# Two batches' states, loaded early and turned on TensorE: one DMA transpose replaced in a hand-ordered kernel

## The chip, the cores and the metric

The kernel runs on one core of a Trainium2 chip. The core has five engines with a queue of their own each: PE (TensorE, the products; its weight loads are shown apart as PEld), DVE (VectorE), ACT (ScalarE), POOL (GpSimd) and SP (SyncE, which here only issues DMAs). The metric is the device time of one execution in microseconds (us), lower is better; of several runs the median is given.

## The reference, cut to what matters

Attention in both directions between a sequence x and a small state, for 8 batches and 8 heads, and behind it a two-layer block with a leaky ReLU:

```python
B, H, S, Ns, D = (8, 8, 512, 32, 64)
scores  = scale * x @ state.T      # per batch and head: 512 x 32
a       = softmax(scores)          # over the 32 state rows
xread   = a @ state
scores2 = scale * state @ x.T      # 32 x 512
a2      = softmax(scores2)         # over the 512 positions
sread   = a2 @ x
rows    = concatenate([xread, sread], axis=2)   # 544 rows a batch, 512 columns (heads side by side)
h       = rows @ w_in              # 4352 x 512 by 512 x 2048
out     = maximum(0.01 * h, h) @ w_out          # 2048 -> 512
```

## The kernel before, in words

**Layout.** The two products `xread = a @ state` and `xread @ w_in` are not made one after the other. For each batch the kernel first makes M = state @ w_in (`a_m`, line 381: heads times states on 256 rows, 2048 columns, in four chunks of 512 columns, each of eight small products), and then h = relu(a @ M) (`ff1`, line 411, 16 blocks j of 128 columns). For both it needs the states transposed, with the head dimension D on the partitions, two heads beside each other: `st_of` (line 214) picks the piece of `stbd` (batch 0), `st1` (batch 1), `st_t[0]` (batches 2 and 3) or `st_t[1]` (batches 4 to 7). The scores (`a_scores`, line 221) are products of the same transposed states with the transposed x (`xT`).

**States.** Batches 0 and 1 are loaded at the start as one DMA of 1-KB rows (`st0f`, line 63: four state rows a partition), scaled, and turned by `state01` (line 157): products whose second operand is a set of columns picked from the identity (`identg`), so that the result stands turned and in the order that the later products want, and two copies on ACT. Batches 2 and 3 (and 4 to 7) go another way: `load_state` (line 177) issues eight DMAs on SP with rows of 256 bytes, and `state_t` (line 186) scales them on POOL and turns them by a DMA transpose on SP into `st_t`. For batches 2 and 3 the load is issued at line 1126, behind a memset on DVE (line 1088) that holds it back, and `state_t(0)` stands at line 1146.

**The head.** x[0] comes in four DMAs, two on SP and two on ACT (line 69), the weights and x[1], x[2] in DMAs issued by POOL. A few products on a tile of zeros (`spin`, line 140) run on PE while the first data come. Batch 0's softmax is made in two halves u = 0, 1 of 256 positions each (`scores0`, `max0`, `rows0`, `split0`, `spread0`, `exp0`, `sum0`, `recip0`, `probs0`, lines 889 to 971). `max0(u, v)` is a reduction on DVE; the negated maxima are split into two bf16 parts (hi, lo) and added to the scores by products; ACT takes the exponential. Then `Quad` (line 1035) makes batch 0's h in half-width blocks, and `piece` (line 693) batch 0's second layer. From batch 1 on, the second layer runs in seven products instead of eight on sums of operands (`Fast`, line 738), whose units are spread between the other work by `before.run(1)` or `u`.

**What sets the order.** The kernel is under a manual schedule: each engine takes its instructions in just the order in which the program writes them, and waits in that order. Lines 973 to 1264 write the order from the start to batch 2 out by hand, `FIRST` (line 1353) that of batch 2's stretch, as a string of short names, and `ORDER` (line 1342) that of batches 3 to 6. So a step that is moved past another changes what is queued behind what. The PSUM banks are handed out by tags with a fixed number of buffers ("big" and "sc" one, "ph" and "py" two): a product that takes a bank waits until the last reader of its former tile is done.

**Around the change.** On PE, line 1179 makes chunk 3 of batch 1's M and line 1182 chunk 0 of batch 2's M, the first product on `st_t[0]`. Batch 1's softmax runs on DVE and ACT from line 1145 (`a_top`, `a_rows`, `a_less`, `a_exp`, `a_max2`, `a_probs`). x[2] and x[3] are cast to bf16 by `cast_x` on ACT and POOL and turned by DMA transposes on SP (`a_xt_dma`, line 208). POOL also makes some of the sums of second-layer weights (`weights_sum`, line 729).

## Time and profile before

| | us |
|---|---|
| median of 3 runs | 201.35 (201.06 to 201.36) |
| the profiled execution | 201.61 |
| its span, first to last instruction | 199.8 |
| PE busy | 193.8 |
| DVE busy | 164.8 |
| ACT busy | 150.1 |
| POOL busy | 63.9 |

How to read the rows that follow. In the order of time a row is: start, duration, engine, line of the kernel, operation, tile written <- tiles read, shape written <- shape read, count; in brackets the idle time of the engine before it and what ended it. `SPq` or `POOL ... DMA_DIRECT2D` rows are the issues of DMAs, not their transfer. A row of the waits is: engine and line <- what it waited for: us in total, times, longest. A row of the DMA issues is: tiles, queue, kind, count, KB in all (a group's mean of one where x8 stands: 16.0 KB each), and the median us from issue to landing. Products are pipelined, so a PE row's duration runs beyond the start of the next; from start to start a product of 512 columns takes 0.22 us here.

### The profile page before, as it was taken

What the parts mean: (1) busy time and instruction counts of PE and PEld (TensorE: products, weight loads), DVE (VectorE), ACT (ScalarE), POOL (GpSimd) and SP (SyncE); (2) the same over time, 40 slices, a digit from 0 to 9 for tenths busy, and PEclk for the clock granted to TensorE, in tenths of its full rate; (3) what the DMA queues carried; (4) which work ended last, traced back from release to release, by engine and by line L of the source; (5) the groups of instructions that cost most, each with busy time, mean ns of one, the idle gap of its engine ahead of it and who ended that gap; (6) DMA issues with size and microseconds to landing.
All of it is one profiled execution on the core that took longest, in us unless ns stands there. A gap on an engine that the chain in (4) does not pass through costs nothing.

```text
span 199.8 us, 5151 instructions
## 1 busy us (share of the span) xinstructions
PE 193.8 (97%) x2106; PEld 136.5 (68%) x2106; DVE 164.8 (82%) x282; ACT 150.1 (75%) x286; POOL 63.9 (32%) x90
## 2 busy tenths in 40 slices
PE   7999998999999999999999999999999999999993
PEld 2566533446677667767777777777777788799882
DVE  2676498599999998997999899999899877995613
ACT  3478628599779649997899779996999768767710
POOL 8473284790009102720413040500050024005350
PEclk9999999999999999999999999999999999999999
DMA  6999997999571998398293614080013401310026
GB/s 203 212 207 192 199 292 136 206 318 162 101 220 27 197 276 165 58 255 268 51 259 113 184 22 85 3 262 0 3 51 159 82 3 76 134 56 0 5 82 182
DMA packets 40616, 27.50 MB, mean 138 GB/s; under 512 B 25424, under 2 KB 37840, under 8 KB 40592
## 3 DMA queue, kind: packets, MB, share of 16 engines
q1 hardware_dynamic: 34032, 20.35, 39.7%
q0 software_dynamic: 5728, 6.03, 16.8%
q10 hardware_dynamic: 832, 0.79, 1.2%
q8 instruction: 16, 0.26, 0.6%
q14 instruction: 8, 0.07, 0.1%
HBM read 17.30 MB, written 8.91 MB: 131 GB/s over the span
## 4 chain that ended last, share of the span: by engine, by line
PE 90%; DMA 4%; DVE 3%; POOL 0%; issue 0%; ACT 0%; ACTq 0%
PE yq L770 43%; PE ph L414 18%; PE pm L393 4%; PE pf L492 3%; PE yu L770 3%; PE pl L660 3%; PE ph L1051 3%; DMA st_t<-stb 2%; DMA xf<-in_x_dram 2%; PE py L699 2%; PE pl L581 2%; PE pyw L699 1%; PE psn L359 1%; PE sc L225 1%; PE php L1051 1%; PE phw L427 1%
## 5 line engine op out<-in xcount | busy, mean ns | idle before, releaser
L420 ACT ACTIVATE hT<-ph 128x512 bf16<-128x512 f32 x84 | 49.1, 608 | 14.3 <-PE ph L414 14.3
L770 PEld LDWEIGHTS <-su 128*128 128x128 bf16 x480 | 46.2, 98 | 12.4 <-ACT hT L420 0.4
L414 PE MATMUL ph<-aT,M 128*128 128x512 bf16 x168 | 47.9, 379 | 0.0
L770 PEld LDWEIGHTS <-hT 128*128 128x128 bf16 x336 | 32.3, 98 | 12.0 <-issue 2.7
L770 PE MATMUL yq<-tw_xf,su 128*128 128x256 bf16 x224 | 30.8, 273 | 0.0
L770 PE MATMUL yq<-w_out_bf,hT 128*128 128x256 bf16 x224 | 29.2, 273 | 0.0
L114 POOL CAST xb<-xl 128x512 bf16<-128x512 f32 (+1 forms) x24 | 15.2, 673 | 20.9 <-DMA xl<-in_x_dram 20.9
L414 PEld LDWEIGHTS <-M 128*128 128x128 bf16 x168 | 16.0, 98 | 7.7 <-issue 1.9
L759 DVE TENSOR_TENSOR su<-hT 128x1024 bf16<-128x1024 bf16 x28 | 19.1, 686 | 2.6 <-ACT hT L420 2.5
L842 POOL TENSOR_TENSOR yo<-sv,sv 128x512 f32<-128x512 f32 x7 | 9.3, 1330 | 37.2 <-ACT e L313 31.4
L1283 ACT CAST M<-pm 128x512 bf16<-128x512 f32 x30 | 16.8, 596 | 0.6 <-PE pm L393 0.6
L779 ACT COPY sv<-yq 128x512 f32<-128x512 f32 x24 | 14.0, 587 | 3.4 <-PE yq L770 3.3
L770 PE MATMUL yq<-tw_x,su 128*128 128x256 bf16 x112 | 16.3, 273 | 0.0
L770 PE MATMUL yq<-w_out_bf,su 128*128 128x256 bf16 x112 | 15.3, 273 | 0.0
L782 DVE TENSOR_TENSOR yo<-yq,sv 128x512 f32<-128x512 f32 x20 | 13.5, 677 | 2.1 <-PE yq L770 2.1
L770 PE MATMUL yq<-tw_x,hT 128*128 128x256 bf16 x104 | 13.9, 273 | 0.0
L313 ACT ACTIVATE e<-sc,mcol 128x512 bf16<-128x512 f32 x16 | 11.2, 704 | 0.2 <-DVE mcol L307 0.2
L699 PEld LDWEIGHTS <-hT 128*128 128x128 bf16 x64 | 5.9, 98 | 7.4 <-issue 0.9
L759 DVE TENSOR_TENSOR su<-su,hT 128x1024 bf16<-128x1024 bf16 x14 | 10.6, 755 | 0.2
L672 ACT COPY ls<-pl 128x512 f32<-128x512 f32 x16 | 9.5, 592 | 1.5 <-PE pl L660 1.0
L307 DVE TENSOR_REDUCE mcol<-sc 128x2 f32<-128x1024 f32 x8 | 9.7, 1216 | 0.0
L235 DVE TRANSPOSE_TENSOR_REDUCE mrow<-sc 128x32 f32<-128x1024 f32 x7 | 8.7, 1243 | 0.5 <-PE sc L225 0.5
(193 smaller groups left out, 350.8 us busy)
## 6 DMA issues: line engine op xcount, KB each, us to landing
xl<-in_x_dram SPq DMA_DIRECT2D x5, 1024.0 KB, 6.6
out_dram<-yo SPq DMA_DIRECT2D x10, 512.0 KB, 2.9
w_in_bf<-in_moe_w_in_dram POOLq DMA_DIRECT2D x4, 512.0 KB, 7.9
out_dram<-yo SPq DMA_DIRECT2D x7, 256.0 KB, 2.7
w_out_bf<-in_moe_w_out_dram POOLq DMA_DIRECT2D x2, 512.0 KB, 12.8
w_out_bf<-in_moe_w_out_dram POOLq DMA_DIRECT2D x4, 256.0 KB, 13.1
xl<-in_x_dram POOLq DMA_DIRECT2D x2, 512.0 KB, 15.4
out_dram<-ysb SPq DMA_DIRECT2D x4, 256.0 KB, 4.0
```

What stands on the lines that cost most here:

```text
L114: copy(xs[b][:, h0 // NK, :, h0 % NK:h0 % NK + h1 - h0].rearrange("p t h d -> p h t d"), xl[b][:, h0:h1].rearrange("p h (t d) -> p h t d", ...
L307: nc.vector.tensor_reduce(out=a.m2[:], in_=a.sc[:], axis=AX.X, op=ALU.max, negate=True)
L313: nc.scalar.activation(out=a.e2[:, g], in_=a.sc[:, g, :], func=AF.Exp, bias=a.m2[:, g:g + 1], accum_out=a.r2[:, g:g + 1],)
L414: nc.tensor.matmul(ph[:], lhsT=a.M[:, g, P * j:P * (j + 1)], rhs=a.aT[:, g, :], start=(g == 0), stop=(g == 1),)
L420: nc.scalar.activation(out=hT[:, j, :], in_=ph[:], func=AF.Prelu, scale=1.0 / SCALE, alpha=0.01)
L672: copy(self.sv[n], flat)
L699: nc.tensor.matmul(y.py, lhsT=hT[:, j, P * i:P * (i + 1)], rhs=w_out_bf[:, j, :], start=(j == 0), stop=(j == 15),)
L759: (eng or nc.vector).tensor_tensor(out=S[n][:, ms], in0=u[:, ms], in1=v[:, ms], op=op)
L770: nc.tensor.matmul(bank[:, i, :], lhsT=lhs[:, m, P * i:P * (i + 1)], rhs=rhs[:, m, :], start=(first and m == 0 and (i == 0 or of is not No ...
L779: copy(t[:], bank)
L782: nc.vector.tensor_tensor(out=dst, in0=bank, in1=self.sv[n][:], op=ALU.add)
L1283: copy(t.M[:, g, DM * c:DM * (c + 1)], src[g][:] if isinstance(src, list) else src[:, g, :])
```

## The change

The states of batches 2 and 3 are loaded like those of batches 0 and 1: one DMA on SP with rows of 1 KB, written right after the first three weight loads, and held back by a two-element memset that now stands on POOL behind those loads. They are scaled on DVE between `max0(1, 0)` and `max0(1, 1)`, turned by eight products with columns of the identity (`heads`) into the bank "sc" after `sum0(0)`, and copied to `st_t[0]` by ACT. The eight DMAs of `load_state(0)`, the scaling on POOL and the DMA transpose of `state_t(0)` are gone. Batches 4 to 7 keep the old way. The products on the tile of zeros (`spin`) stay as they are.

The helpers are cut into smaller ones (`split0` into `hi0` and `lo0`, and so on), and the orders written by hand are new ones. In the head up to the quads only few steps change places. Further on, evictions move between ACT and DVE, pieces and units change places, chunk 0 of batch 2's M comes ahead of chunk 3 of batch 1's, the first cast of x[3] on POOL comes ahead of `weights_sum(0, 4, 8)`, a part of `load_state(1)` comes ahead of the transposes of batch 0's second probabilities and of x[3], and `FIRST` is another string. `ORDER` is unchanged.

```diff
+    def load_x1(u):
+        nc.gpsimd.dma_start(
+            a1.xb[:, NK * u:NK * (u + 1)].rearrange("p h t d -> p h (t d)"),
+            x[1, NK * u:NK * (u + 1)].rearrange("h (p t) d -> p h (t d)", t=NT),
+        )
...
-    stf = [consts.tile([P, hi - lo, P], FP32, name=f"stf{lo}", tag=f"stf{lo}") for lo, hi in groups]
-    stb = [consts.tile([P, hi - lo, P], BF16, name=f"stb{lo}") for lo, hi in groups]
+    shapes = ([P, 4, D], [P, 4, P])
+    stf = [consts.tile(shapes[i], FP32, name=f"stf{i}", tag=f"stf{i}") for i in range(2)]
+    stb = [consts.tile(shapes[i], BF16, name=f"stb{i}") for i in range(2)]
+    pst = []
+
+    def load_state23():
+        nc.sync.dma_start(
+            stf[0][:], state[2:4].rearrange("b h n d -> (b h n) d").rearrange("(p r) d -> p r d", r=4)
+        )
+
+    def scale_state23(eng):
...
+            eng.tensor_scalar(out=stb[0][:], in0=stf[0][:], scalar1=SCALE, scalar2=None, op0=ALU.mult)
+
+    def place_state23(tag):
+        ps = psum.tile([P, 4, D], FP32, name="pst2", tag=tag, bufs=1)
+        for r in range(4):
+            for g in range(2):
+                nc.tensor.matmul(
+                    ps[D * g:D * (g + 1), r, :], lhsT=stb[0][:, r, :], rhs=heads[:, :, :, g],
+                    start=True, stop=True,
+                )
+        pst.append(ps)
+
+    def take_state23(copy):
+        copy(
+            st_t[0][:].rearrange("p b (k q r) -> p (b k) q r", k=NK, r=4),
+            pst[0][:].rearrange("p r (h q) -> p h q r", q=8),
+        )
...
-            nc.vector.memset(stf[0][:, 0, D - 1:D + 1], 0.0)
...
+    load_w_in(0)
+    load_w_in(1)
+    load_w_in(2)
+    nc.gpsimd.memset(stf[0][:, 0, D - 2:D], 0.0)
+    load_state23()
+    cast_x0(0, 0, 4, VEC)
...
+    scores0(1, 0)
+    max0(1, 0)
+    scale_state23(nc.vector)
+    rows0(1)
+    spread0(scn[0], hi[0], False, False)
+    spread0(scn[0], lo[0], False)
+    exp0(0)
+    scores0(1, 1)
+    max0(1, 1)
...
+    sum0(0)
+    place_state23("sc")
+    take_state23(SCA)
+    hi0(1)
+    lo0(1, nc.vector)
+    recip0(0)
+    spread0(scn[1], hi[1], False, False)
...
-    load_state(0)
     m_make(a1, 1, "ph")
     a_scores(a1)
+    m_take(a1, 1, 0, VEC)
...
-    state_t(0)
-    a_rows(a1)
     a_less(a1)
     a_exp(a1)
-    m_take(a1, 2, 1, SCA)
...
+    m_take(a1, 2, 0, VEC)
+    m_take(a1, 2, 1, VEC)
+    a_max2(a1)
...
     cast_x(3, 0, 2, POO)
...
+    weights_sum(0, 4, 8, nc.gpsimd)
+    a_exp2(a1, 1)
+    m_make(a2, 0, "sc")
+    cast_x(3, 2, 4, POO)
     m_make(a1, 3, "ph")
...
+    y_store(0, 0, SCA)
+    ff(5)
...
+    ff(6, "big")
+    a_xt_dma(att_of[3])
+    relu.pop(5)()
     relu.pop(4)()
+    ff(8)
```

## The prediction

> **What bounds the kernel now.** I read the page's first part, then the list of what TensorE (PE) waited for, then the chain of waits around the one long wait in that list, and last the order of time in the first 13 us, where the change puts its new work.

> ```profile
> PE 193.8 (97%) x2106; PEld 136.5 (68%) x2106; DVE 164.8 (82%) x282; ACT 150.1 (75%) x286; POOL 63.9 (32%) x90
> ```

> PE is busy 193.8 of 199.8 us. An engine this full leaves two ways for the time to move: PE gets more or less work, or it loses or gains a wait. So I look at its waits.

> ```profile
> PE pspin L143 <- DVE warm L76: 1.2, 1, 1.2
> PE pm L393 <- DMA st_t<-stb: 1.0, 1, 1.0
> PE pxth L877 <- DVE xb L121: 0.2, 1, 0.2
> ```

> Only the second can be won by this change: a product on the transposed states of batches 2 and 3. The chain of waits says what stood before it, and the order of time shows PE's last work before and its first after.

> ```profile
> 29.77 0.87 POOL stb L187
> 30.66 4.37 DMA st_t<-stb
> 33.70 0.41 PE L393 MATMUL pm<-w_in_bf,st 64*32 64x512 bf16 x8
> 35.07 0.41 PE L393 MATMUL pm<-w_in_bf,st_t 64*32 64x512 bf16 x8 [0.96 <-DMA st_t<-stb]
> ```

> The states are scaled on POOL, turned by a DMA transpose that lands 4.37 us after its issue, and PE stands still for 0.96 us. Behind this point PE runs without a listed wait almost to the end, so about 1.0 us is all that the removal can bring.

> **The change part by part.** *Removed:* eight small state DMAs, one scaling on POOL (0.87 us), one DMA transpose. None but the last is waited for, and POOL and SP have time to spare; the eight DMAs took bandwidth, and what they give back comes to loads that already land ahead of use. Value: the 1.0 us above.

> *Added on PE and ACT:* eight products of 64 columns, and one copy. The trace has their like in `state01`, with 96 columns:

> ```profile
> 3.54 0.55 DVE L864 TENSOR_SCALAR stb<-st0f 128x256 bf16<-128x256 f32 x1 [2.41 <-DMA st0f<-in_state_dram]
> 4.28 0.40 PE L161 MATMUL pst<-identg,stb 128*64 128x96 bf16 x8
> 4.61 0.82 PE L143 MATMUL pspin<-idle 128*128 128x512 bf16 x3
> 4.72 0.37 ACT L165 CAST stbd<-pst 128x256 bf16<-128x256 f32 x1 [1.04 <-PE pst L161]
> ```

> From 4.28 to the next product at 4.61 is 0.33 us for 96 columns; 64 columns cost no more, at least 0.2 us. The ACT copy is 0.37 us and the scaling, now on DVE, 0.55 us.

> *The new wait.* This is the term that decides. `scale_state23` stands on DVE between `max0(1, 0)` and `max0(1, 1)`, and DVE takes its instructions in order. If the state has not landed, DVE stands, and queued behind it are `max0(1, 1)`, `hi0(1)`, `lo0(1)`, `recip0(0)`, and through them the second half of the softmax of batch 0 and PE. The rows of that place before the change:

> ```profile
> 8.42 0.42 DVE L927 TENSOR_REDUCE m<-sct 128x8 f32<-128x256 f32 x1
> 9.54 0.42 DVE L927 TENSOR_REDUCE m<-sct 128x8 f32<-128x256 f32 x1 [0.70 <-PE sct L892]
> 9.98 0.25 PE L953 MATMUL r<-ones,e 128*128 128x4 bf16 x4
> 10.35 0.41 PE L918 MATMUL scn<-ident,hi 128*32 128x128 bf16 x16
> ```

> DVE is free from 8.84 to 9.54, so a scaling of 0.55 us is free if the state has landed by about 9.0. Each us later is one us later for 9.54, and PE has nothing else to run after 9.98 (`place_state23` itself waits for the scaled state and for the bank "sc", which `max0(1, 1)` frees). So when does it land? The DMA is issued on SP, but behind a wait for a memset that stands on POOL after three weight loads:

> ```profile
> 3.07 2.50 POOL L127 DMA_DIRECT2D w_in_bf<-in_moe_w_in_dram  x3
> ```

> Those end at 5.57; with the memset (some 0.1 us) the issue comes at about 5.7. For issue to landing the trace has two neighbours, the states of batches 0 and 1 at the very start, and the eight small state loads at 19.62, which stand in the list of DMA issues:

> ```profile
> st0f<-in_state_dram ACTq DMA_DIRECT2D x1, 128.0 KB, 2.8
> stf<-in_state_dram SPq DMA_DIRECT2D x8, 16.0 KB, 5.0
> ```

> The first has the same shape as the new load (128 rows of 1 KB) and took 2.8 us; the second is an eighth of it and took 5.0 us. What differs is the traffic beside them. Below: the first issue of the small loads, the two queues from 19 to 23.3 us, and in the last row the POOL queue from 5.6 to 9 us, where the new load falls (packets, MB, share of the 16 engines' time):

> ```profile
> 19.62 3.63 SPq L181 DMA_DIRECT2D stf<-in_state_dram  x8
> ...
> q0 software_dynamic: 1341, 0.85, 135.4%
> q1 hardware_dynamic: 3, 0.00, 0.1%
> ...
> q0 software_dynamic: 665, 0.66, 120.0%
> ```

> With the POOL queue (q0) keeping all 16 DMA engines full, SP's queue (q1) moved 3 packets in 3.7 us after its first issue. From 5.6 us q0 is just as full (over 100%, since packets overlap). So the bounds are 5.7 + 2.8 = 8.5 and 5.7 + 5.0 = 10.7, and I take the second, the row with the same queue, source and neighbour traffic, plus 0.1 for a larger transfer: **landing at 10.8**. [...]

> Landing 10.8, scaling to 11.35: `max0(1, 1)` starts at 11.35 instead of 9.54, **1.8 us later**. The place products and their copy then lie in PE's and ACT's wait and cost nothing more. PE is back to back from 13 us on, so nothing takes the 1.8 us back.

> *Reordering, 13 to 52 us.* Two places can turn into waits. First the chain of batch 1: two evictions of `m_make(a1, 2)` move from ACT to DVE, ahead of `a_max2(a1)`.

> ```profile
> 28.48 1.22 DVE L248 TENSOR_TENSOR sh<-sc,mrowb 128x1024 f32<-128x1024 f32 x1
> 29.63 1.21 DVE L307 TENSOR_REDUCE mcol<-sc 128x2 f32<-128x1024 f32 x1
> 33.46 0.88 DVE L274 TENSOR_TENSOR aT<-e,qb 128x1024 bf16<-128x1024 bf16 x1
> 35.62 0.59 ACT L1107 CAST M<-pm 128x512 bf16<-128x512 f32 x1 [0.37 <-PE pm L393]
> 35.86 0.59 PE L414 MATMUL ph<-aT,M 128*128 128x512 bf16 x2
> ```

> Two evictions at about 0.6 us put `aT` of batch 1 at 34.34 + 1.2 = 35.5. Without its wait PE reaches `ff(0)` at 33.70 + 0.56 (two sets of eight, 48.59 to 49.15 in the row below) + six products of 0.22 us = 35.6. So it just fits: 0 to 0.2 us. Further on `ff(8)` may wait for `relu.pop(4)`, now behind a copy and another relu on ACT, each as in the ACT row above: 0 to 0.5 us, by which of the two "ph" banks it gets. I take 0.1 for both together.

> Second, the transpose for batch 3. On POOL the first cast of x[3] now stands ahead of `weights_sum(0, 4, 8)`, so three casts come after it:

> ```profile
> 40.62 2.14 POOL L736 TENSOR_TENSOR tw_xf<-w_out_bf 128x1024 bf16<-128x1024 bf16 x1
> 42.78 2.28 POOL L114 CAST xb<-xl 128x512 bf16<-128x512 f32 x4
> 45.87 1.87 SPq L209 DMA_TRANSPOSE xT<-xb  x1
> DMA to landing us min/median/max: 6.0/6.0/6.0
> 48.59 0.63 PE L393 MATMUL pm<-w_in_bf,st_t 64*32 64x512 bf16 x16
> 49.15 1.05 PE L770 MATMUL yq<-w_out_bf,hT 128*128 128x256 bf16 x8
> 52.43 0.40 PE L225 MATMUL sc<-xT,st_t 64*32 64x512 bf16 x8
> ```

> x[3] lands by 42.78, where its casts start; taken so, they end at 42.78 + 2.28 + 2.14 = 47.2 instead of 45.06. The transpose, issued at 45.87 before, goes at 47.2 and lands by 51.9 + 1.3 = 53.2 at worst (6.0 us), or some 51.5 if it goes faster without the stores that ran beside it. PE wants it at 52.43 before; after, at 52.43 + 1.8 - 1.0 + 0.1 = 53.3. With the late head it is free; with an early one it bites (second rival).

> **The sum:** +1.8 (new DVE wait) - 1.0 (transpose wait gone) + 0.0 (place products, in the wait) + 0.1 (reordering) = **+0.9 us**. The profiled execution took 201.6 us (span 199.8 and 1.8 around it), the median of three runs is 201.35; on the median that gives **202.3 us**.

> **The rivals.** *The state lands in time (faster).* If q1 gets its turn as at the start of the kernel, the state is there at 8.5, the scaling fits between 8.84 and 9.54, and only the place products (0.2) stand against the 1.0: 201.35 - 0.8 = 200.55, with up to 0.6 of it lost to the reordering, so about 200.85. It decides at a landing of 9.0 for the full gain and about 9.9 for break-even. For it speaks the 2.8 us of the equal shape, and that q0 had only begun; against it the 5.0 us and the 3 packets. [...]

> *The gain is eaten (same).* With an early or middling landing PE wants batch 3's transpose at 52.43 - 0.7 = 51.7 and finds it between 51.5 and 53.2: up to 1.0 us lost again. Or the state lands near 9.9. Either gives about 201.35.

> *The state waits far longer.* The 5.0 us come from a q0 with smaller rows before it; three weight loads of 512 KB queued at 5.6 us may hold q1 longer. Landing at 13 gives +2.2 more, 204.

> That the change does not do what it says (PE still waits at that product) would need another late input: `a_exp2(a1, 1)` must free the bank "sc". ACT's inputs move by the same 1.2 us of DVE, but ACT was held by a cast before, and I find it done near 33.5, just ahead of PE's 33.7. This costs 0 to 0.2 and lies inside the other cases.

> **How the numbers follow.** Forecast 0.58, in time 0.24, eaten 0.13, far longer 0.05. A measurement of this kernel tells 0.2% (0.4 us) from no change. Faster by more than that: 0.24; within: 0.14; slower: 0.62. Range: the forecast's own is 201.8 to 203.2 (landing 10.3 to 11.7). For 8 in 10 it must reach most of the faster case too: 200.7 to 203.2.

> **What would show each step right or wrong.** Right: the list of PE's waits has a new one near 10 us, on DVE or through it on the state's DMA, of 1.5 to 2 us, DVE shows a wait on that DMA before the scaling, the state load lands 4.5 to 5.5 us after issue, and the wait on `st_t` is gone. Wrong: the load lands in under 3.3 us and DVE does not stand; then look for a wait on `xT` near 51 us and for ACT around 41 us.

## The result, and the profile after

The changed kernel takes **203.76 us** (median of 5 runs, 202.83 to 204.13) where the kernel before takes 201.35 in the same comparison (201.06 to 201.42): a ratio of 1.0119, interval 1.0094 to 1.0144. That is +2.4 us; the forecast was +0.9, and 203.76 lies outside its range. Profiled execution against profiled execution it is 203.76 against 201.61, +2.15 us, and spans of 202.0 against 199.8; the account below is made on these.

The page of the changed kernel, first part, and the list of what TensorE waited for:

```profile
PE 193.7 (96%) x2092; PEld 137.6 (68%) x2114; DVE 164.8 (82%) x284; ACT 149.2 (74%) x285; POOL 61.0 (30%) x90
```

```profile
PE pst L200 <- DVE m L962: 2.0, 1, 2.0
PE pspin L149 <- DVE warm L76: 1.2, 1, 1.2
PE ph L449 <- issue: 0.5, 3, 0.2
```

The wait for `st_t` is gone and a wait of 2.0 us at the place products has come. (The third row is taken for no wait: the page has 2092 products against 2114 weight loads, so it probably stands where records of products are missing.) What stood behind the new one is in the same list for VectorE, in the list of DMA issues, and in the order of time:

```profile
DVE stb L194 <- DMA stf<-in_state_dram: 2.5, 1, 2.5
```

```profile
stf<-in_state_dram SPq DMA_DIRECT2D x1, 128.0 KB, 5.7
```

```profile
5.60 0.10 POOL L1093 MEMSET stf<- 128x2 f32 x1
5.74 0.35 SPq L186 DMA_DIRECT2D stf<-in_state_dram  x1
...
10.16 0.25 PE L980 MATMUL r<-ones,e 128*128 128x4 bf16 x4
11.55 0.53 DVE L194 TENSOR_SCALAR stb<-stf 128x256 bf16<-128x256 f32 x1 [2.53 <-DMA stf<-in_state_dram]
12.00 0.40 DVE L962 TENSOR_REDUCE m<-sct 128x8 f32<-128x256 f32 x1
12.45 0.43 PE L200 MATMUL pst<-ident,stb 128*64 128x64 bf16 x8 [2.04 <-DVE m L962]
12.81 0.62 PE L953 MATMUL scn<-ident,hi 128*32 128x128 bf16 x16
```

Read from top to bottom this is the predicted wait: the memset holds the issue until 5.74, the load lands 5.71 us later (11.45), DVE stands 2.53 us, `max0(1, 1)` starts at 12.00 where it started at 9.54, and PE goes on at 12.81 where it went on at 10.35. That is **+2.46 us**, not 1.8.

But PE's durations have changed as well. The `scn` row takes 0.62 us; the same product took 0.41. The windows of the changed kernel, cut where the granted clock changes, at 12.29 and 15.70 us, and in two steps of the same 3.41 us ahead of that (columns: stretch, its length, busy time of PE, PEld, DVE, ACT, POOL, then the granted clock, DMA share, GB/s), and the window of the kernel before at the same place:

```profile
5.46:8.87 3.41, 3.31 (x56) 1.91 (x57) 2.76 (x11) 1.50 (x2) 0.88 (x4) 1.00 1.23 204
8.87:12.29 3.42, 1.49 (x52) 1.00 (x45) 0.89 (x3) 1.18 (x2) 3.42 (x6) 1.00 1.22 219
12.29:15.70 3.41, 3.25 (x77) 2.05 (x77) 2.16 (x7) 1.00 (x3) 2.15 (x4) 0.50 1.24 207
```

```profile
7.81:11.23 3.42, 3.18 (x128) 2.17 (x120) 2.62 (x9) 1.42 (x4) 2.63 (x5) 1.00 1.24 204
```

From 12.29 to 15.70 us, 3.41 us long, PE's clock is granted at 0.50. The stretch ahead of it is the one with the wait: PE is busy 1.49 of 3.42 us in it, where before it was busy 3.18. The price can be read from products that both traces have. First the kernel before, then the changed one:

```profile
12.75 0.41 PE L918 MATMUL qb<-ident,q 128*32 128x128 bf16 x16
25.02 0.44 PE L225 MATMUL sc<-xT,st 64*32 64x512 bf16 x8
39.40 0.41 PE L225 MATMUL sc<-xT,st_t 64*32 64x512 bf16 x8
```

```profile
16.14 0.41 PE L953 MATMUL qb<-ident,q 128*32 128x128 bf16 x16
28.39 0.43 PE L260 MATMUL sc<-xT,st 64*32 64x512 bf16 x8
41.62 0.41 PE L260 MATMUL sc<-xT,st_t 64*32 64x512 bf16 x8
...
54.61 0.40 PE L260 MATMUL sc<-xT,st_t 64*32 64x512 bf16 x8
```

At the second `qb` the changed kernel is 3.39 us behind (16.14 - 12.75), 0.93 more than at `scn`: the half clock. At the scores of batch 1 it is still 3.37 behind, at those of batch 2 only 2.22: over the place where the wait for `st_t` was, 1.15 us came back (a wait of 0.96 us, and what the new order moved there). At the scores of batch 3 it is 2.18 (54.61 against the 52.43 of the prediction's row), and so it stays to the end. 2.46 + 0.93 - 1.15 - 0.04 = +2.2, the difference of the spans.

### The profile page after: what moved, and what is told of

It reads as the page before. It is cut to its first block, busy times and chain, and to the rows that moved or that the text cites. A ratio compares the mean times of both kernels' runs of the same rounds, so it can differ in the third digit from the quotient of the medians.

```text
span 202.0 us, 5132 instructions
## 1 busy us (share of the span) xinstructions
PE 193.7 (96%) x2092; PEld 137.6 (68%) x2114; DVE 164.8 (82%) x284; ACT 149.2 (74%) x285; POOL 61.0 (30%) x90
## 4 chain that ended last, share of the span: by engine, by line
PE 91%; DMA 3%; POOL 2%; issue 1%; DVE 1%; POOLq 0%; DVEq 0%
PE yq L805 43%; PE ph L449 17%; PE pm L428 4%; PE pyw L734 4%; PE py L734 3%; PE pf L527 3%; PE yu L805 3%; PE pl L695 3%; PE ph L1031 3%; DMA stf<-in_state_dram 3%; PE pl L616 2%; POOL w_in_bf L127 1%; PE sc L260 1%; PE psn L394 1%; PE php L1031 1%
## 5 line engine op out<-in xcount | busy, mean ns | idle before, releaser
L449 PE MATMUL ph<-aT,M 128*128 128x512 bf16 x149 | 44.3, 379 | 0.8 <-issue 0.5
L877 POOL TENSOR_TENSOR yo<-sv,sv 128x512 f32<-128x512 f32 x7 | 9.1, 1298 | 40.8 <-ACT e L348 24.5
L114 POOL CAST xb<-xl 128x512 bf16<-128x512 f32 (+1 forms) x24 | 13.2, 586 | 15.8 <-DMA xl<-in_x_dram 15.8
L1358 ACT CAST M<-pm 128x512 bf16<-128x512 f32 x31 | 17.4, 596 | 0.7 <-PE pm L428 0.6
L814 ACT COPY sv<-yq 128x512 f32<-128x512 f32 x23 | 13.4, 586 | 2.6 <-PE yq L805 2.5
L290 ACT ACTIVATE e<-sh 128x1024 bf16<-128x1024 f32 x7 | 7.4, 1058 | 3.8 <-DVE sh L283 3.8
L794 DVE TENSOR_TENSOR su<-su,hT 128x1024 bf16<-128x1024 bf16 x14 | 9.6, 687 | 0.3
```

What stands on the lines that cost most here:

```text
L114: copy(xs[b][:, h0 // NK, :, h0 % NK:h0 % NK + h1 - h0].rearrange("p t h d -> p h t d"), xl[b][:, h0:h1].rearrange("p h (t d) -> p h t d", ...
L449: nc.tensor.matmul(ph[:], lhsT=a.M[:, g, P * j:P * (j + 1)], rhs=a.aT[:, g, :], start=(g == 0), stop=(g == 1),)
L794: (eng or nc.vector).tensor_tensor(out=S[n][:, ms], in0=u[:, ms], in1=v[:, ms], op=op)
L814: copy(t[:], bank)
L1358: copy(t.M[:, g, DM * c:DM * (c + 1)], src[g][:] if isinstance(src, list) else src[:, g, :])
```

## The experiments

The theory after the result: the late state makes DVE and PE stand, the standing halves PE's clock, and the removed wait gives 1.15 us back. The rival for each: the rest of the change (place products, new order) costs it, or the 1.15 us have another source. Every kernel was timed beside the kernel before on the same chip; the last, e15, has one run. The medians of the kernel before were 201.44, 201.47, 201.32 and 201.40 in the four groups.

**1. Fill the wait (e3_fill).** The half clock is taken away and the wait left. The nine products add zeros to columns that nobody reads; for that the tile of the sums, `r0`, is made 512 columns wide (`r0w`):

```diff
...
     sum0(0)
+    for _ in range(9):
+        nc.tensor.matmul(r0w[1][:, NG:], lhsT=idle[:, :P], rhs=idle[:, NG:], start=False, stop=False)
     place_state23("sc")
```

> Nine products of 496 columns on the tile of zeros stand on PE behind sum0(0), ahead of the place products, where PE waits 2.0 us; they add zeros to columns that nobody reads. Theory: DVE's wait stays (2.5 us), PE has no gap, the granted clock stays full, and the half clock's price is won back: 202.6 to 203.1. Rival (the half clock is a symptom without a price, since PE waits for others there anyway): 203.5 to 204.

Measured 202.81 us, ratio 1.0072 (1.0045 to 1.0100). In the order of time and in its list of cores:

```profile
10.82 2.04 PE L1148 MATMUL r<-idle 128*128 128x496 bf16 x9
...
13.04 0.41 PE L953 MATMUL scn<-ident,hi 128*32 128x128 bf16 x16
...
15.44 0.41 PE L953 MATMUL qb<-ident,q 128*32 128x128 bf16 x16
```

```profile
core 0: 201.5 us, clock 1.000
```

Adding nine useless products made the kernel 0.95 us faster. The two rows of its trace say where: from this `scn` to the second `qb` e3 takes 2.40 us, as the kernel before does (12.75 - 10.35), and the changed kernel 3.33 (16.14 - 12.81), with the clock at 1.000 in e3. DVE's wait for the state is still there, 2.1 us in this trace. So the half clock is shown, and its price of 0.93 us with it. (Five of e3's eight runs lie at 202.76 to 202.83; the other three, the profiled one among them, took 203.29 to 204.37 at full clock, and why is not known.) The runs of the changed kernel say the same: four had a mean clock of 0.989 to 0.992 and took 203.52 to 204.13, the one with 1.000 took 202.83.

**2. Take the wait away (e2_nowait, e1_late, e4_gate_first).** Three ways. e2 lets the scale read another tile that is already there (`st0f`, so batches 2 and 3 compute with wrong states); e1 moves the scale behind `a_max2(a0)` and products and copy behind `turn(1)`; e4 keeps all in place and issues the load earlier:

```diff
-            eng.tensor_scalar(out=stb[0][:], in0=stf[0][:], ...
+            eng.tensor_scalar(out=stb[0][:], in0=st0f[:], ...
```

```diff
-    scale_state23(nc.vector)
...
-    place_state23("sc")
-    take_state23(SCA)
...
     a_max2(a0)
+    scale_state23(nc.vector)
...
     turn(1)
+    place_state23("sc")
+    take_state23(SCA)
```

```diff
+    nc.gpsimd.memset(stf[0][:, 0, D - 2:D], 0.0)
+    load_state23()
     load_w_in(0)
     load_w_in(1)
     load_w_in(2)
-    nc.gpsimd.memset(stf[0][:, 0, D - 2:D], 0.0)
-    load_state23()
```

> The scaling reads the states of batches 0 and 1 (landed at 3.5 us) in place of those of batches 2 and 3; their load is still issued, and nobody waits for it. Batches 2 and 3 are so computed with the wrong states; every instruction and its place is the changed kernel's. Theory: DVE's wait of 2.5 us gone, PE's place products fall into its gap before hi0(1), clock full: 200.2 to 200.7. Rival (place or traffic of the load, the products or the order cost the time): 202 or more.

> The scaling moves on DVE to behind a_max2(a0), the place products and their copy to behind turn(1), near 24 us; all else is the changed kernel. Theory (a wait of DVE for the state's landing, 2.5 us, and behind it 3.4 us of PE at half clock, about 0.9 us; the order itself costs nothing): both waits gone, granted clock full from 5.5 us on, no wait on st_t at 35 us, the place products about 0.3 us on PE: 200.3 to 200.8. Rival (the new order or the new products cost the time, and the wait only replaces others): at least 202.

> The memset and the state load stand ahead of the three weight loads, so the issue comes near 3.2 us, before POOL's queue has begun to move data. Theory (5.7 us from issue to landing come from the full POOL queue): it lands in under 4.5 us, before 7.7 us, DVE does not wait; x[0]'s last piece may land up to 0.4 us later; 200.4 to 201.1. Rival (the load takes over 5 us in any place, by its path or its source): over 5 us from issue to landing, about 8.5 us; the time could still fall. If the time stays over 202, the wait was not the cause.

Measured: e2 201.96 (ratio 1.0017, 0.9993 to 1.0042), e1 201.40 (1.0011, 0.9984 to 1.0037), e4 201.41 (1.0002, 0.9980 to 1.0024). The order of time of e4:

```profile
3.33 0.34 SPq L186 DMA_DIRECT2D stf<-in_state_dram  x1
...
9.04 0.28 DVE L194 TENSOR_SCALAR stb<-stf 128x256 bf16<-128x256 f32 x1
...
9.83 0.42 DVE L962 TENSOR_REDUCE m<-sct 128x8 f32<-128x256 f32 x1 [0.50 <-PE sct L928]
```

Issued 2.4 us earlier, the load lands at 6.88, the scale runs in DVE's free time and `max0(1, 1)` waits for its own input again. All three are 1.8 to 2.4 us faster than the changed kernel, so the DVE wait and what hangs on it are the loss, to within the 0.5 us by which e2's median still lies above that of before. But none gains what the removed wait was to bring: by the medians the change without the new wait is worth 0.0, not -1.0, and the theory's ranges for all three (200.2 to 200.7, 200.3 to 200.8, 200.4 to 201.1) were missed. One more thing can be read in e1's windows:

```profile
8.25:11.67 3.42, 2.31 (x91) 1.51 (x92) 1.79 (x7) 0.99 (x2) 2.98 (x5) 1.00 1.22 218
11.67:15.08 3.41, 2.28 (x76) 1.28 (x64) 1.47 (x4) 1.50 (x4) 2.36 (x4) 1.00 1.24 208
```

In this execution (203.73 us, the slowest of e1's twelve) weight loads came late and PE stood 1.11 and 0.99 us; with 2.31 of 3.42 and 2.28 of 3.41 us busy the clock stayed. So the half clock followed a stretch at 44% (1.49 of 3.42) and did not follow these at 67%; e15 below narrows it.

**3. Is it the new order that eats the gain? (e5 to e8).** e5 has the new order with the old state path; e6 and e7 the old order with the new path, e6 at the changed kernel's places, e7 at e1's; e8 leaves the head alone:

```diff
-    load_state(0)
+    load_state23()
...
     piece(0, h0, 0, 1, copy=None, part=(2, 3))
+    place_state23("ph")
+    take_state23(SCA)
...
-    state_t(0)
+    scale_state23(nc.gpsimd)
```

> The changed kernel's new order of the steps, with the state's old path (state_t's DMA transpose at its old relative place, no product with identity columns, no scale on DVE in the head). It keeps the wait of about 1.3 us of TensorE for st_t near 35 us and has no wait of DVE near 9 us, so TensorE's clock should stay at 1.0 there. Theory A (the new order costs what the changed kernel with the state in time failed to gain, about 1.0 us): 202.2 us (201.9 to 202.8). Theory B (the new order is free, as predicted): 201.4 to 201.6, the same as before.

> The order of the steps of before, with the changed kernel's state: load, scale behind the first max, place and take where the changed kernel has them. DVE's wait of 2.5 us and the half clock behind it should both be there. Theory B (order free): 203.5 us, like the changed kernel (203.0 to 203.9). Theory A (order costs 1.0): 202.6 us.

> The order of before, the changed kernel's load, but the scale behind a_max2(a0) and the products and the take behind a_exp2(a0, 1): the state has landed by then, so there is no wait of DVE, no idle TensorE near 10 us, and no wait of TensorE for st_t near 35 us. Theory A (it was the new order that ate the gain in the twin with the new order, 201.40): 200.5 us (200.1 to 200.9). Theory B (something else ate it: the wait for st_t is not worth its 1.0 us, or the load of the state delays the head): 201.4 us (201.0 to 201.8).

> The order of before and a head without the state: the 1-KB-row load is issued at the place of the old one near 20 us, scaled on POOL where state_t stood, turned by the identity products some steps later, read off by ACT before a_exp2(a1, 1). The DMA transpose is gone and nothing is added to the first 20 us. If the wait for st_t near 35 us is worth its 1.0 us: 201.4 - 1.0 + 0.35 (eight products and a read-off) = 200.75 us (200.4 to 201.1). If that wait only moves to another place: 201.4 us (201.1 to 201.8).

Measured: e5 201.95 (1.0031, 1.0004 to 1.0058), e6 204.24 (1.0124, 1.0076 to 1.0171), e7 201.18 (0.9978, 0.9958 to 0.9998), e8 201.36 (0.9991, 0.9968 to 1.0015). The old order does not rescue the changed kernel (e6 is no faster than it), so the order is no part of its loss. With the head on time the order may cost something: 0.1 to 1.2 us in e5, and 0.2 between e7 and its twin e1, where the intervals overlap; e4 and its twin e11 below show nothing. But e8, with the old order, the head untouched and the wait for `st_t` gone, was to gain 0.7 us and gained 0.1 (-0.6 to +0.3). Theory A of these runs explains a part at most. e7 is the fastest version that computes the reference, 0.3 us (0.04 to 0.85) below the kernel before.

**4. What is the old wait worth? (e9 to e12).** Now the kernel before itself, with one thing changed. e9 takes the wait away and nothing else (batch 2 then computes with batch 1's state), e10 makes it longer, e12 is e9 in the new order, and e11 is e4 in the old order:

```diff
-        t = st1 if a.b == 1 else st_t[0][:, a.b - 2] if a.b < 4 else ...
+        t = st1 if a.b in (1, 2) else st_t[0][:, a.b - 2] if a.b < 4 else ...
```

```diff
         nc.gpsimd.tensor_scalar(out=stb[i][:], in0=stf[i][:], scalar1=SCALE, ...
+        if i == 0:
+            nc.gpsimd.tensor_scalar(out=stb[i][:], in0=stf[i][:], scalar1=SCALE, ...
```

> The kernel before with one tile exchanged: batch 2's products with the memory take batch 1's state (st1, ready since the head) in place of st_t, so batch 2 computes with a wrong state. Every instruction, load and transpose stays; only TensorE's wait for st_t near 35 us goes (batch 3 still uses st_t, tens of us later). If that wait sits on the path with its 1.0 us: 201.45 - 1.0 = 200.45 us (200.2 to 200.8). If steps behind it take up what it gives back: 201.2 to 201.5 us.

> The kernel before with the scale of batch 2 and 3's states on POOL issued twice (same values): the DMA transpose starts 0.86 us later, and POOL has 1.7 us free behind it. If TensorE's wait for st_t is on the path: 201.45 + 0.86 = 202.3 us (202.0 to 202.6). If steps behind it have slack that takes up a part: 201.5 to 201.9 us.

> The new order of the steps with the old state path, and batch 2 reading st1 in place of st_t (a wrong state, no wait near 35 us): the fourth corner beside the kernel before, the new order alone (201.95) and the old order without the wait. If order and wait are independent and both on the path: 201.95 - 0.8 = 201.15 us (200.8 to 201.5). If the new order takes up what the wait gives back: 201.7 to 202.1 us.

> The order of before, the 1-KB-row load issued ahead of the three weight loads (landing near 6.9 us instead of 11.4), scale, products and take where the changed kernel has them. No DVE wait, no half clock, no wait for st_t. If the new order costs 0.2 to 0.5 us (as its run alone says): 200.9 to 201.2 us. If the old order gives nothing here: 201.4 us, like the same load in the new order. Fast enough, this would be the best version that does what the change does.

Measured: e9 201.06 (0.9986, 0.9973 to 0.9999), e10 201.29 (0.9994, 0.9980 to 1.0007), e12 201.32 (1.0005, 0.9987 to 1.0022), e11 201.46 (1.0006, 0.9988 to 1.0025). So a step of 0.86 us added ahead of the wait costs nothing, and the wait taken away alone brings 0.3 us, not 1.0. In the new order the same removal is worth 0.6 us by the medians (e12 against e5, with intervals that overlap), inside the range set for two independent effects. e11 missed its 200.9 to 201.2: the old order gives e4 nothing. Why the removal brings so little is, for e9, in its order of time:

```profile
38.96 0.41 PE L225 MATMUL sc<-xT,st 64*32 64x512 bf16 x8 [0.47 <-DMA xT<-xb]
```

PE runs through the old wait and stands at the scores of batch 2, now for `xT`. In the kernel before `xT` landed at 38.80 and PE came at 39.40, so the next input had only 0.6 us of slack.

That reason holds only where the DMA transpose of the states stays. In the traces of e4, e7 and e8, which turn them on PE, `xT` lands sooner (at 37.83 in e4), and PE does not wait for it at batch 2. Two rows of e4, then one of e8:

```profile
10.70 0.41 PE L953 MATMUL scn<-ident,hi 128*32 128x128 bf16 x16
...
38.80 0.41 PE L260 MATMUL sc<-xT,st_t 64*32 64x512 bf16 x8
```

```profile
10.30 0.41 PE L948 MATMUL scn<-ident,hi 128*32 128x128 bf16 x16
```

From this `scn` to the end of the span the kernel before takes 189.5 us (199.8 - 10.35), and e4, e7 and e8 take 188.7 each (199.4 - 10.70, 199.7 - 10.96, 199.0 - 10.30). So in these single executions they are some 0.8 us ahead behind the head, and stay ahead. In e4 and e7 the head itself is late, by 0.35 and 0.61 us; in e8, profiled in the fastest of its twelve runs (200.81), it is not. But e10, which keeps the transpose, takes 188.6 as well (199.3 - 10.71): its head is 0.36 us late, its `st_t` lands sooner, and its wait is 0.17 us. So the 0.96 us are the wait of one execution and no fixed price. That it is shorter in most others would explain why the medians gain so little; it is not shown.

Why e10 costs nothing is in its order of time, POOL, SP and PE:

```profile
30.02 0.86 POOL L187 TENSOR_SCALAR stb<-stf 128x256 bf16<-128x256 f32 x1
30.96 0.85 POOL L189 TENSOR_SCALAR stb<-stf 128x256 bf16<-128x256 f32 x1
...
31.84 1.26 SPq L190 DMA_TRANSPOSE st_t<-stb  x1
...
34.64 0.41 PE L395 MATMUL pm<-w_in_bf,st_t 64*32 64x512 bf16 x8 [0.17 <-DMA st_t<-stb]
```

The transpose goes 1.18 us later than before and lands at 34.60, 0.43 us earlier. Its landing does not follow its issue.

**5. A late head alone, and what holds the transpose (e13 to e15).** e13 is the kernel before with its head made late by ten products of zeros behind `sum0(0)`, as in e3; e14 the same with e9's exchange; e15 is the kernel before with the last weight load moved:

```diff
-    load_w_out(3, 2)
+    load_w_out(3, 2, (12,))
...
     state_t(0)
+    load_w_out(3, 2, (14,))
```

> The kernel before with ten products of zeros (496 columns each, 2.07 us at 0.207) on TensorE behind sum0(0) near 10 us: the head comes 2 us late and nothing else is changed; st_t is still turned by the DMA transpose. If the wait for st_t is slack that a late head takes up: 201.4 + 2.05 - 1.0 to 0.5 = 202.4 to 203.0 us, and no wait for st_t in the profile. If the wait moves with the head: 203.4 us (203.2 to 203.7).

> The same late head, and batch 2 reads batch 1's state (st1, a wrong state for batch 2), so nothing in the first 50 us waits for st_t. If a late head takes up the wait by itself, the removal is worth nothing here: equal to the late head alone within 0.2 us. If the removal has a worth of its own: 0.5 to 1.0 us faster than the late head alone.

> The kernel before with the last load of w_out (j = 14, 15) issued behind state_t(0) instead of in the queue near 21 us: the weight loads of the head end 1.3 us earlier, the transpose of the states is issued as before. Read from the landing alone. If the end of the weight loads holds st_t back: st_t lands near 33.7 us, some 0.3 us behind the load that is now last. If the transpose takes its 4.4 us anyhow: 35.0 us. DVE's weights_sum(2, 4, 8) will wait for the late load, so the time itself may be longer (201 to 204 us) and tells nothing.

Measured: e13 202.70 (1.0065, 1.0050 to 1.0080), e14 203.05 (1.0081, 1.0068 to 1.0094). How late the head is can be read from the two `scn` rows, first of the kernel before, then of e13:

```profile
8.57 0.41 PE L918 MATMUL scn<-ident,hi 128*32 128x128 bf16 x16
```

```profile
9.02 0.41 PE L918 MATMUL scn<-ident,hi 128*32 128x128 bf16 x16
...
12.73 0.41 PE L918 MATMUL scn<-ident,hi 128*32 128x128 bf16 x16
```

From the first to the second it is 1.78 us before (10.35 - 8.57) and 3.71 in e13, so the products make the head 1.93 us late. That costs the old kernel 1.3 us (1.0 to 1.6), some 0.6 less than it is late, and in e13's list of PE's waits there is none for `st_t`:

```profile
PE pspin L143 <- DVE warm L76: 1.2, 1, 1.2
PE pxth L877 <- DVE xb L121: 0.3, 1, 0.3
```

Taking the cause of the wait away beside the late head (e14) brings nothing more; its median is 0.35 us higher, more than the 0.2 us that its expectation allowed, with intervals that overlap. So the late head takes up the old wait by itself, whether the transpose is there or not. e15 took 202.80 us in its one run, with DVE behind the late load as expected, and PE behind `st_t`. The rows on the end of the weight loads and on `st_t`, first of the kernel before, then of e15:

```profile
34.90 0.69 DVE L736 TENSOR_TENSOR tw_x<-w_out_bf 128x1024 bf16<-128x1024 bf16 x1 [0.56 <-DMA w_out_bf<-in_moe_w_out_dram]
```

```profile
31.55 1.27 SPq L188 DMA_TRANSPOSE st_t<-stb  x1
...
35.91 0.69 DVE L736 TENSOR_TENSOR tw_x<-w_out_bf 128x1024 bf16<-128x1024 bf16 x1 [1.24 <-DMA w_out_bf<-in_moe_w_out_dram]
...
36.21 0.41 PE L393 MATMUL pm<-w_in_bf,st_t 64*32 64x512 bf16 x8 [1.59 <-DMA st_t<-stb]
```

Neither number of the expectation came: the moved load did not leave the stretch, it landed later (35.78), and `st_t` came behind it at 36.16. Its window at this wait, cut in steps of 3.41 us counted on from 6.44 us (its mean clock is 1.000, so no change of the clock marks a step here), also says more of the clock:

```profile
33.75:37.16 3.41, 1.82 (x22) 0.56 (x21) 2.03 (x4) 1.81 (x5) 0.06 (x1) 1.00 1.15 205
37.16:40.57 3.41, 3.41 (x24) 1.41 (x22) 1.59 (x3) 1.73 (x4) 3.09 (x2) 1.00 0.94 249
```

PE stood 1.59 us, was busy 1.82 of 3.41 us (53%), and kept its clock. What happens between 44% and 53% these traces do not show. The landings of the traces together, one trace for each kernel, in us:

| kernel | transpose issued | last load of w_out landed | st_t landed | issue to landing |
|---|---|---|---|---|
| before | 30.66 | 34.77 | 35.03 | 4.37 |
| e9 | 30.65 | 34.88 | 35.14 | 4.49 |
| e12 | 30.57 | 34.34 | 34.60 | 4.03 |
| e5 | 31.15 | 34.20 | 34.55 | 3.40 |
| e10 | 31.84 | 34.22 | 34.60 | 2.76 |
| e15 | 31.55 | 35.78 | 36.16 | 4.61 |
| e14 | 32.54 | 34.34 | 34.94 | 2.40 |
| e13 | 32.97 | 33.83 | 35.37 | 2.40 |

In the first six `st_t` lands 0.26 to 0.38 us behind the last load of POOL's queue, whatever its issue; in the last two, issued late enough, it takes 2.40 us from its issue. By these traces the wait at 35 us was the end of the weight loads, not the length of the transpose.

## Why the prediction was wrong

The direction, the place and the mechanism were right: the new DVE wait, the state's load behind the full POOL queue, the place products inside the wait, and the end of the `st_t` wait are all in the trace. The size was not. Step by step:

- **"Landing at 10.8 ... 1.8 us later."** Mis-sized. Issue was 5.74 as worked out, but issue to landing took 5.71 us, not the 5.0 of the chosen row: landing 11.45, and +2.46 at `scn`. The neighbour's 5.0 us was taken as the value where it was a hint of the kind: in the six traces with the load at this place it took 5.7 to 6.4 us, and at the neighbour's own place, in e8, 5.45. The 0.1 us for a larger transfer was the author's estimate; no run shows it. e4's load, issued at 3.33 beside the first weight load (3.24), took 3.55 us.
- **"PE has nothing else to run ... cost nothing more."** This step failed. That the products in the wait are free is right (from the end of `max0(1, 1)` to `scn` it is 0.41 us, 0.39 before). What was left out is that PE, idle for 2.04 us, ran slower behind the wait: 0.93 us for 3.41 us at half clock, shown by e3. The profile of before had its clock at 1.00 there, and the sum had no term for it. This is the larger of the two missing amounts (the landing's is 2.46 - 1.8 = 0.66), and it decided: the one run of the changed kernel that kept the full clock took 202.83, inside the range.
- **"-1.0 (transpose wait gone)."** Right in the sum (-1.15 in the trace), wrong in its reason and so in the rivals. The wait was slack of the loads that a late head takes up by itself (e13 against e14). The changed kernel's head is later still, so there the removal itself most likely brought nothing, though no run puts the old transpose back into it; that -1.15 came out near -1.0 is then luck. With the head on time the medians show 0.0 to 0.3 us (e4, e7, e8, e9); in e9 `xT` of batch 2 is late next, and the wait itself, 0.96 us in the execution that the prediction read, was 0.17 in e10's. The sentence "about 1.0 us is all that the removal can bring" named a bound; it was used as the value, and what is late next was looked for at batch 3 and not 4 us further on.
- **"+0.1 (reordering)."** -0.04 in the trace; batch 3's transpose is not waited for. With an early head e5 puts the new order at 0.1 to 1.2 us, e4 against e11 at nothing.
- **The rivals.** "The state lands in time" was tried by e4, where the state is there at 6.88: 201.41, not 200.85. Its trace is 0.8 us ahead behind the head, but its head is 0.35 us late, and the rest is open as said. By these medians its break-even, a landing at 9.9, was too late. (In the third rival 2.2 us more than the forecast's 202.3 is 204.5, not 204.)

The sum with the measured terms: 2.46 + 0.93 - 1.15 - 0.04 = +2.2, against +2.15 between the profiled executions and +2.4 between the medians. What stays open besides is under 0.5 us: how the loads' end moves from run to run (33.8 to 34.9 in the table's traces with the loads in their old places), and whether e5's cost has one place; its trace has two waits of 0.2 us near 70 and 80 us, on ACT and DVE, that the trace of before lacks.

## What to carry to other kernels

Price a new wait on a full PE twice: by its length, and by what the clock does behind it. Here a wait of 2.04 us in a stretch of 3.42 us at 44% busy was followed by a half clock that cost 0.93 us, and one of 1.59 us in a stretch at 53% was not; nine idle products in the wait made the kernel 0.95 us faster (e3). Before counting a removed wait as a gain, look for the next input of the same engine and for what really ended the wait: a transfer that lands right behind a queue of loads (0.26 to 0.38 us behind it in six traces here) may be late because of the loads. Two terms of opposite sign, a later head and a wait behind it, are not independent: the first may take up the second (in e13 a head 1.93 us late cost 1.3 us, and the wait was gone). And the wait of one profiled execution need not be that of the others: look at a second trace before it is put into a sum.
